# Where the query features of two tiles are made, which engine stores the gates, and one raw buffer fewer, in a fused gMLP and linear-attention kernel

## The chip, the cores and the metric

The kernel runs on one core of a Trainium2 chip. The metric is the time of one execution on the device, in microseconds (us). The core has TensorE (PE in the profile; its weight loads are PEld), VectorE (DVE), ScalarE (ACT), GpSimd (POOL) and SyncE (SP). Each engine has its own stream of instructions; they meet at semaphores. SP, ACT and POOL also start DMA transfers.

## What is computed

The reference, cut to what matters, with S = 2048 rows, D = 512 columns, H = 32 heads of 16, and 688 gated channels:

```python
xn = layernorm(x)
# A: linear attention
q, k, v = split_heads(xn @ wqkv)
phi(t) = concat(softmax(t @ w_phi), softmax(-(t @ w_phi)))      # per head, 32 features
o = phi(q) (phi(k)^T v) / (phi(q) sum(phi(k)) + 1e-6)
A = merge_heads(o) @ wo
# B: gated MLP with a spatial projection
z1, z2 = split(gelu(xn @ w_in))                                 # 688 + 688 channels
g = w_sp @ layernorm(z2) + b_sp                                 # over the 2048 rows
B = (z1 * g) @ w_out
return x + A + B
```

All is float32; each product of matrices is made of three matmuls over operands split into a rounded part and a rest.

## The kernel before

Rows are worked in 16 tiles of 128. A **pair** is two neighbouring tiles. The kernel has four stages.

1. **Attention inputs** (to about 200 us): layernorm, the projections of q, k and v, the two softmaxes of each. The unnormalised features of q (`e`, 128 x 1024 a tile, with the reciprocals of their sums) are stored to the DRAM tensor `e_d`; the raw z1 halves go to `z1_d`.
2. **Gate inputs** (to about 275 us): the sum of the key features `zb`, the z2 half with its gelu and layernorm, and the B operands of the spatial product. The **finished features** of tiles 0 and 1 (`NE = 2`) are made here: `q_fin` (lines 559 to 570) multiplies `e` by `zb`, sums per head (L563, L564), makes the quotient (L565 to L568) and scales `e` by it (L570). They go back to `e_d`.
3. **Spatial stage** (its products from 275 to 484 us): `w_sp @ z2` by Strassen-Winograd on 2 x 2 blocks. There are 8 pairs of output tiles, and each is worked in 4 **chunks**, so chunks 0 to 31. A chunk has seven products, P1, P2, P6, P5, P7, P3, P4, of six matmuls each of 344 columns (lines 57 to 59); the seven accumulate over the four chunks of a pair in seven PSUM buffers `g` of a pool of eight. In what follows 12P2 is product P2 of chunk 12.
4. **Output stage** (from about 484 us): for every pair of tiles the gated u times `w_out`, the attention by finished features, and its product with `wo`.

**What one chunk costs the other engines.** `load_a(n)` has SP load 512 KB of `w_sp` into a raw buffer `wf` (L607). `prep_a(n)` makes the left operands from it: ACT rounds (L49), DVE subtracts for the rest (L53) and forms the Winograd sums (L637 to L640). An A operand has four tiles: A11 with A12 (used by P1 and P2), A22 (P4), S2 with S1 (P6 and P5), S4 with S3 (P7 and P3). There are two sets of them, for even and odd chunks, so the tiles of chunk n + 2 are written only after the products of chunk n that read them.

**What one pair costs.** After the last chunk of pair i `drain` empties the seven `g` into `c`: ACT copies P1 (L835), DVE does the other seven steps (L834, L837, L838, L840). The next pair's P2 takes the buffer that P1 held, its P6 that of P2, and so on. `gate` applies gelu to z1, which POOL has loaded into `z1t` (L808, L850 on ACT), multiplies it by `c` (L853 on DVE), and `turn` transposes the product in 32 x 32 blocks into the same `z1t` (L862, L864) and stores it to DRAM (L868, L870), eight DMAs a pair. `c` and `z1t` have one buffer each.

**Turned features.** The attention wants the finished features transposed. For pair 0 (tiles 0, 1) and pairs 4 to 7 (`TQ = 8`) DVE transposes them in blocks and POOL stores them to `q_d` (`turn_q`, L579, L581), from where they are loaded turned. Tiles 0 and 1 are turned in the spatial stage after the gates of pairs 2 and 4: `e` comes into the buffer of `c`, its transpose goes to that of `z1t` (L966 to L968). Pairs 1 to 3 (tiles 2 to 7) are transposed by PE (`attend_T`, L1047, into `ptq`) and copied by ACT (L1049). Tile 2 is finished at chunk 29, tiles 3 to 15 in the output stage (`features`, from `ahead(i)`, three tiles ahead).

**What sets the order.** A scheduler orders each engine's instructions when the kernel is built, by times that it estimates; on the chip each engine then takes its instructions in that order. `in_turn` (L647) fixes by hand the order of named steps of DVE and ACT where the stages meet (chunks 1 to 8).

```python
if n + 4 < NC:
    raw[n + 4] = load_a(n + 4)          # three raw buffers: f, x, y
if 0 < n < NC - 2:
    A[n + 2] = prep_a(n + 2, raw.pop(n + 2))
```

Of the kernel before, what the change touches and what calls it, by code (L numbers as in the profile page):

```python
# [18 lines left out]
P = 128  # L19
# [22 lines left out]
def mixer(ctx: ExitStack, tc: tile.TileContext, x, x_t, wv, wqkT, phi_bd, wo, w_in, wst, b_r, w_out, out):  # L42
# [528 lines left out]

    TQ = 8

# [27 lines left out]
    def load_a(n):  # L601
        i, q = SEQ[n]
        tag = "fx"[n] if n < 2 else "fxy"[(n - 2) % 3]
        t = (fy[0] if tag == "y" else ws).tile([P, 2, QC, P], F32, tag="wf" + tag, name="wf")
        for k in range(2):
            with tc.issue_after(load_a.last) if n == 5 else ExitStack():
                load_a.last = sp.dma_start(t[:, k], wst[2 * i + k, :, q * QC:(q + 1) * QC, :]).ins  # L607
        return [t[:, k].rearrange("p (k two) t -> p two k t", two=2) for k in range(2)]
# [38 lines left out]
    def in_turn(*keys):  # L647
        for e in range(2):
            queue = [turns[k][e] for k in keys if e < len(turns[k])]
            for a, b in zip(queue, queue[1:]):  # L650
                tc.add_manual_dep(b, a.name, mybir.DependencyInfo(
                    mybir.DependencyClass.NoSync, mybir.DependencyReason.DATA), reason="order of the border")
# [177 lines left out]
    def drain(i, g, cb):  # L830
# [12 lines left out]
        for k, x in enumerate(steps + [drained]):  # L843
            turns["c", i, k] = x.ins,
        return cb, first.ins, drained.ins

    def gate(i, cb, z, u, ut, after=None):
        cb, first, _ = cb
        with tc.issue_after(after or first):
            act.activation(z[:, :, :FH], z[:, :, :FH], AF.Gelu_apprx_tanh)  # L850
        zs = z[:, :, :FH].rearrange("p k (j f) -> p k j f", j=2)
        us = u[:, :, :FH].rearrange("p k (j f) -> p k j f", j=2)
        dve.tensor_tensor(us, zs, cb, op=ALU.mult)  # L853
        lo, hi = u[:, :, KF * P:FH], u[:, :, FH:FU].bitcast(F32R)
# [3 lines left out]
        def turn():  # L858
            src = ut.rearrange("p k f -> p (k f)")
            m, r = src[:, :2 * KF * P], src[:, 2 * KF * P:]  # L860
            for k in range(2):
                dve.transpose(m[:, k * KF * P:(k + 1) * KF * P].rearrange("p (m c t) -> p m c t", c=KF, t=BL),  # L862
                              u[:, k, :KF * P].rearrange("p (c m j) -> p m c j", c=KF, j=BL))
            dve.transpose(r.rearrange("p (k f) -> p k f", k=2), u[:, :, KF * P:])  # L864
            eng = pool if i == NP - 2 else sp
            for b in range(0, P, BL):
# [51 lines left out]
    for n in range(NC):  # L918
# [5 lines left out]
        if n % NQ == NQ - 1 and i < NP - 1:  # L924
# [3 lines left out]
            g = {}  # L928
        if n + 4 < NC:
            raw[n + 4] = load_a(n + 4)  # L930
        if 0 < n < NC - 2:
            A[n + 2] = prep_a(n + 2, raw.pop(n + 2))
        if n == 6:
            in_turn((1, "sums"),
# [24 lines left out]
        if n % NQ == NQ - 1 and i < NP - 1:  # L959
            turn = gate(i, cb, z, c, z, prep_a.last)  # L960
            if i < NP - 2:
                turn()
            if i in (2, 4):
                s = i // 2 - 1
                e, t = (gt.tile([P, 2, FU], F32, tag=tag, name=name).rearrange("p k f -> p (k f)")[:, :NF]
                        for tag, name in (("c", "c"), ("z1", "z1t")))  # L966
                pool.dma_start(e, e_d[s, :, :NF])
                turn_q(s, t, e, pool)  # L968
        if n == NC - 4:
            stage_w()  # L970
        if n == NC - 3:
            zb = slot("zb")[:, :NF]
            sp.dma_start(zb, zb_d)
            uT = [first_gate(0)]
            ets[2] = load_q(2, slot("et"))
            es[2], last = q_fin(ets.pop(2), slot("qtmp")[:, :NF], zb)
        if n == NC - 2:
# [25 lines left out]
    def features(s):  # L1003
        with tc.issue_after(fin[-1]):
            tmp = slot("qtmp")[:, :NF]
# [117 lines left out]
    with tc.issue_after(load_w.last):  # L1123
        ets[3] = load_q(3, slot("et"))
        for s in (2, 3):
            us[s] = fetch_u(s)
        ets[4] = load_q(4, slot("et"))

    def ahead(i):

        if i + 5 < NT:
            ets[i + 5] = load_q(i + 5, slot("et"))
        if i + 4 < NT:
            with tc.issue_after(brought[i + 2]) if i + 6 >= NT else ExitStack():
                us[i + 4] = fetch_u(i + 4)
        if 3 < i + 3 < NT:
            features(i + 3)

    p, nxt = {}, dict(enumerate(uT))
    for i in range(0, NT, 2):  # L1140
# [65 lines left out]
```

## Time and profile before

| | |
|---|---|
| Median of 3 runs | 611.46 us (611.17 to 613.96) |
| The profiled execution | 612.24 us, of which the span of the instructions is 610.5 us |
| Busy in the span: PE, PEld, DVE, ACT, POOL | 99%, 90%, 86%, 43%, 22% |
| Mean granted clock of TensorE | 1.000 |
| DVE busy, 300 to 340 us, 340 to 380, 500 to 540 | 37.45, 32.99, 38.90 of 40 us |
| Data moved | 107.85 MB, 177 GB/s on average |

How to read it: times are microseconds from the span's start, means of a group are nanoseconds. In a group's row the numbers are busy time and mean, then the time that the engine stood idle just before these instructions and what ended most of it. In a timeline a row is an instruction with its start and duration; the idle time ahead of it, where there was any, stands in brackets with what ended it. Instructions of one engine overlap a little, so the distance between two starts is what one costs when the next doesn't wait. A busy PE is not PE at its peak, since matmuls are pipelined; the count of matmuls in a window says more.

### The profile page before, as it was taken

How to read it: one execution, taken by the hardware profiler on the slowest of the kernel's cores; microseconds unless marked ns; L12 is line 12 of the kernel's file. 1: busy time of each engine (PE TensorE's matmuls, PEld its weight loads, DVE VectorE, ACT ScalarE, POOL GpSimd, SP SyncE). 2: the span in 40 equal slices, each digit the busy share in tenths (PEclk: the TensorE clock that was granted, in tenths of full speed). 3: DMA queues.
4: the chain of work that ended last, by engine and by line, in shares of the span. 5: the costliest groups of instructions: out<-in, count | busy, mean ns of one | idle time of the engine just before them, and what ended most of it. 6: DMA issues, size and time to landing. Idle time of an engine off the chain costs nothing.

```text
span 610.5 us, 11382 instructions
## 1 busy us (share of the span) xinstructions
PE 602.8 (99%) x4286; PEld 548.5 (90%) x4286; DVE 525.4 (86%) x930; ACT 260.3 (43%) x414; POOL 131.8 (22%) x231
## 2 busy tenths in 40 slices
PE   8999999999999999999999999999999999999997
PEld 7888888888888999999999999999999988877775
DVE  5999999999987578989999897997998999999922
ACT  5643324423433547877434433443435343332220
POOL 4122332323111005442000001001100041153420
PEclk9999999999999999999999999999999999999999
DMA  8557876566537758002344736556664799699782
GB/s 315 193 130 178 217 176 188 145 168 165 144 96 221 241 201 306 5 1 65 121 107 135 208 104 173 163 154 161 176 185 154 228 299 292 191 326 248 183 236 67
DMA packets 57950, 107.85 MB, mean 177 GB/s; under 512 B 12392, under 2 KB 24552, under 8 KB 57672
## 3 DMA queue, kind: packets, MB, share of 16 engines
q1 hardware_dynamic: 43656, 65.22, 34.6%
q0 software_dynamic: 11936, 36.28, 24.2%
q10 hardware_dynamic: 2304, 5.64, 2.4%
q8 instruction: 33, 0.54, 0.4%
q14 instruction: 21, 0.17, 0.1%
HBM read 66.85 MB, written 35.54 MB: 168 GB/s over the span
## 4 chain that ended last, share of the span: by engine, by line
PE 82%; DVE 5%; ACT 4%; issue 4%; POOL 3%; DMA 1%; ACTq 0%; POOLq 0%; DVEq 0%
PE g L57 9%; PE g L59 9%; PE g L58 9%; PE proj L58 7%; PE proj L57 7%; PE proj L59 7%; PE pout L57 5%; PE pout L59 5%; PE pout L58 5%; PE zps L57 3%; PE zps L59 3%; PE zps L58 3%; PE po L1062 1%; DMA et<-e_d 1%; PE kvps L372 1%
## 5 line engine op out<-in xcount | busy, mean ns | idle before, releaser
L57 PE MATMUL g<-B,A 128*128 128x344 f32 x448 | 140.4, 317 | 0.9 <-ACT A L49 0.9
L58 PE MATMUL g<-B,A 128*128 128x344 f32 x448 | 141.1, 317 | 0.0
L59 PE MATMUL g<-B,A 128*128 128x344 f32 x448 | 135.5, 317 | 0.0
L49 ACT ACTIVATE A<-wf 128x512 fp32r<-128x512 f32 (+1 forms) x128 | 69.9, 573 | 109.5 <-DVE wf L639 64.8
L57 PEld LDWEIGHTS g<-B,A 128*128 128x128 f32 x448 | 83.8, 188 | 1.4 <-ACT A L49 1.4
L53 DVE TENSOR_TENSOR A<-wf,A 128x512 fp32r<-128x512 f32 (+1 forms) x128 | 76.5, 619 | 9.8 <-ACT A L49 9.4
L58 PEld LDWEIGHTS g<-B,A 128*128 128x128 f32 x448 | 84.0, 188 | 0.0
L59 PEld LDWEIGHTS g<-B,A 128*128 128x128 f32 x448 | 82.7, 188 | 0.3 <-DVE A L53 0.2
L57 PE MATMUL proj<-wqk_h,xT 128*128 128x512 f32 x128 | 50.1, 391 | 0.0
L59 PE MATMUL proj<-wqk_h,xT 128*128 128x512 f32 x128 | 49.8, 389 | 0.0
L58 PE MATMUL proj<-wqk_l,xT 128*128 128x512 f32 x128 | 49.8, 389 | 0.0
L124 ACT ACTIVATE e<-e,r_x 128x1024 f32<-128x1024 f32 x26 | 29.7, 1148 | 42.2 <-DVE e L123 41.2
L57 PE MATMUL zps<-w1h,xT 128*128 128x344 f32 (+2 forms) x128 | 40.9, 320 | 0.0
L59 PE MATMUL zps<-w1h,xT 128*128 128x344 f32 (+2 forms) x128 | 40.7, 318 | 0.0
L58 PE MATMUL zps<-w1l,xT 128*128 128x344 f32 (+2 forms) x128 | 40.7, 318 | 0.0
L57 PE MATMUL zps<-w2h,xT 128*128 128x344 f32 (+2 forms) x128 | 40.7, 318 | 0.0
L58 PE MATMUL zps<-w2l,xT 128*128 128x344 f32 (+2 forms) x128 | 40.6, 317 | 0.0
L59 PE MATMUL zps<-w2h,xT 128*128 128x344 f32 (+2 forms) x128 | 40.3, 317 | 0.0
L127 DVE TENSOR_REDUCE sm<-e 128x64 f32<-128x1024 f32 x26 | 31.1, 1199 | 2.5 <-ACT e L124 2.5
L808 POOL DMA_DIRECT2D z1t<-z_d x16 | 9.1, 594 | 105.3 <-DVE A L53 38.2
L57 PE MATMUL pout<-wu,uh 128*128 128x512 f32 x75 | 30.4, 406 | 0.0
L59 PE MATMUL pout<-wu,ul 128*128 128x512 f32 x75 | 29.3, 391 | 0.0
(217 smaller groups left out, 1373.0 us busy)
## 6 DMA issues: line engine op xcount, KB each, us to landing
wf<-in_wst SPq DMA_DIRECT2D x64, 256.0 KB, 3.8
e_d<-e POOLq DMA_DIRECT2D x16, 544.0 KB, 4.4
et<-e_d SPq DMA_DIRECT2D x16, 544.0 KB, 7.1
z_d<-z1f ACTq DMA_DIRECT2D x16, 344.0 KB, 2.9
z1t<-z_d POOLq DMA_DIRECT2D x16, 344.0 KB, 4.2
zacc<-e POOLq DMA_DIRECT2D x10, 512.0 KB, 4.8
u<-u_d SPq DMA_DIRECT2D x15, 320.0 KB, 4.9
xt<-in_x SPq DMA_DIRECT2D x16, 256.0 KB, 4.3
```

The lines of the kernel that those rows point to most:

```text
L49: return act.activation(h, src, AF.Copy).ins
L53: return (eng or dve).tensor_tensor(l, src, h.bitcast(F32), op=ALU.subtract).ins
L57: pe.matmul(dst, ah, bh, start=start, stop=False)
L58: pe.matmul(dst, ah, bl, start=False, stop=False)
L59: return pe.matmul(dst, al, bh, start=False, stop=stop).ins
L124: softmax_pair.last = less, act.activation(e, e, AF.Exp, scale=scale).ins
L127: dve.tensor_reduce(sm, heads(e), axis=AX.X, op=ALU.add)
L372: i = pe.matmul(kv_acc[k:k + QP, m // 4], vs[:, m * QP:(m + 1) * QP], e[:, m * HP:(m + 1) * HP], start=first and m < 4 and len(ready) == n ...
L808: pool.dma_start(t[:, k, :FH], z1_d[2 * i + k])
L1062: lasts[3] = pe.matmul(po[r][c * QP:(c + 1) * QP, k], kvT[rows, m // 2, cols], fs[m // 4][rows, m // 2 % 2], start=True, stop=True).ins
```

## The change

- **Features of tiles 2 and 3** are made and turned in the spatial stage. After the gates of pairs 1, 2, 3 and 4 come tiles 2, 0, 3 and 1. For tiles 2 and 3 `q_fin` runs there too, on `e` in the buffer of `c`, with scratch in that of `z1t` and with `zs`, a copy of `zb` that POOL loads at chunk 6. `TQ` becomes 6: pair 3 (tiles 6, 7) is turned by DVE and loaded turned like the pairs behind it, and pair 1 is loaded turned from `q_d`. Only pair 2 is left to PE's transposes. Tile 4 is finished at chunk 29; the output stage makes tiles 5 to 15, five tiles ahead.
- **One raw buffer fewer.** `zs` takes the third raw buffer, so from chunk 8 on two alternate, and the load of chunk n + 4 stands behind the preparation of chunk n + 2.
- **Stores of the gates**: POOL issues them for pairs 0 to 6, where SP did for pairs 0 to 5.
- **Orders**: at the border pair 0's copy of P1, its gelu, its gate's product and its transposes get fixed places, the last behind the preparation of chunk 7. From chunk 8 on only one thing is fixed: a chunk's S4 rest stands ahead of the next chunk's first sum on DVE.

```diff
-    TQ = 8
+    TQ = 6
...
-        tag = "fx"[n] if n < 2 else "fxy"[(n - 2) % 3]
+        tag = "fx"[n] if n < 2 else "fxy"[(n - 2) % 3] if n < 8 else "fx"[n % 2]
...
-            eng = pool if i == NP - 2 else sp
+            eng = pool if i < NP - 1 else sp
...
-        if n + 4 < NC:
+        if n < 6:
             raw[n + 4] = load_a(n + 4)
         if 0 < n < NC - 2:
             A[n + 2] = prep_a(n + 2, raw.pop(n + 2))
+        if 6 <= n < NC - 4:
+            raw[n + 4] = load_a(n + 4)
+        if n == 6:
+            zs = fy[0].tile([P, 2, QC, P], F32, tag="wfy", name="zs").rearrange("p a b c -> p (a b c)")
+            pool.dma_start(zs, zb_d)
...
-                    (6, "A11"), (6, "A22"), (6, "first"), (6, "sums"), (6, "S2"), (6, "S4"),
+                    (6, "A11"), (6, "A22"), ("z", 0), (6, "first"), (6, "sums"), (6, "S2"), (6, "S4"),
+                    ("u", 0),
                     (7, "A11"), (7, "A22"), (7, "first"), (7, "sums"), (7, "S2"), (7, "S4"),
+                    ("ut", 0, 0), ("ut", 0, 1),
...
-            if i in (2, 4):
-                s = i // 2 - 1
-                e, t = (gt.tile([P, 2, FU], F32, tag=tag, name=name).rearrange("p k f -> p (k f)")[:, :NF]
+            if 0 < i < 5:
+                s = (2, 0, 3, 1)[i - 1]
+                e, t = (gt.tile([P, 2, FU], F32, tag=tag, name=name).rearrange("p k f -> p (k f)")
                         for tag, name in (("c", "c"), ("z1", "z1t")))
-                pool.dma_start(e, e_d[s, :, :NF])
+                t = t[:, :NF]
+                if s < NE:
+                    e = e[:, :NF]
+                    pool.dma_start(e, e_d[s, :, :NF])
+                else:
+                    e, _ = q_fin(load_q(s, e[:, :QW], pool), t, zs)
                 turn_q(s, t, e, pool)
...
-            ets[2] = load_q(2, slot("et"))
-            es[2], last = q_fin(ets.pop(2), slot("qtmp")[:, :NF], zb)
+            ets[4] = load_q(4, slot("et"))
+            es[4], last = q_fin(ets.pop(4), slot("qtmp")[:, :NF], zb)
...
+    for n in range(8, NC - 6):
+        in_turn((n, "S4"), (n + 1, "first"))
...
-        if 3 < i + 3 < NT:
-            features(i + 3)
+        if 0 < i < NT - 5:
+            features(i + 5)
```

**The order that it makes.** Before, on DVE where pair 2 is drained into `c_4071`: `wf_3885` is chunk 12's raw buffer, `wf_3949` chunk 13's, and the `g` of L834 to L840 are the pair's products.

```order
L640 TENSOR_TENSOR wf_3885<-wf_3885 128x2x128
L53 TENSOR_TENSOR A_4016<-wf_3885,A_4016 128x2x256
L834 SCALAR_TENSOR_TENSOR c_4071<-g_3843,bias_78,c_4071 128x344
L53 TENSOR_TENSOR A_4013<-wf_3885,A_4013 128x2x256
L53 TENSOR_TENSOR A_4085<-wf_3949,A_4085 128x2x256
L837 TENSOR_TENSOR c_4071<-g_3850,c_4071 128x344
L838 TENSOR_TENSOR c_4071<-g_3857,c_4071 128x344
L834 SCALAR_TENSOR_TENSOR c_4071<-g_3864,bias_78,c_4071 128x344
L840 TENSOR_TENSOR c_4071<-g_3864,c_4071 128x344
```

The drain stands among the last steps of chunk 12's preparation, ahead of nearly all of chunk 13's. Now, on DVE at the same drain (`c_4088`): `wf_3982` is chunk 13's raw buffer, `c_3838` holds the `e` of tile 2 and is the same single buffer as `c_4088`.

```order
L640 TENSOR_TENSOR wf_3982<-wf_3982 128x2x128
L53 TENSOR_TENSOR A_4100<-wf_3982,A_4100 128x2x256
L53 TENSOR_TENSOR A_4097<-wf_3982,A_4097 128x2x256
L563 TENSOR_TENSOR z1t_3839<-c_3838,zs_3751 128x1024
L564 TENSOR_REDUCE c_3838<-z1t_3839 128x64
L565 TENSOR_TENSOR c_3838<-c_3838 128x64
L566 SCALAR_TENSOR_TENSOR c_3838<-c_3838 128x32
L567 RECIPROCAL c_3838<-c_3838 128x32
L568 TENSOR_TENSOR c_3838<-c_3838 128x64
L570 TENSOR_TENSOR c_3838<-c_3838 128x1024
L579 STREAM_TRANSPOSE z1t_3839<-c_3838 128x1024
L834 SCALAR_TENSOR_TENSOR c_4088<-g_3860,bias_78,c_4088 128x344
```

The whole preparation of chunk 13 and the features of tile 2 now stand ahead of the drain of pair 2. At the drain of pair 4 it is the same with chunk 21 and tile 3; at those of pairs 3 and 5 only the transpose (L579) of tiles 0 and 1 stands just ahead. On PE the scheduler has moved products too: a chunk's P4 comes early, and between the last matmul of 7P4 and the first of 12P2 stand 204 matmuls; from the last of 11P4 to 12P2 stand 36, from 12P2 to 14P4 84, from 14P4 to 14P6 23, from 16P2 to 18P6 104 with 19P4 at 102, and from 18P6 to 20P2 64.

Before, on POOL from the load of pair 2's z1 to that of pair 4's:

```order
L808 DMA z1t_3904<-z1_d_64 128x688 x2
L967 DMA c_4114<-e_d_63 128x1024
L581 DMA q_d_69<-z1t_4115 32x4x256 x4
L808 DMA z1t_4190<-z1_d_64 128x688 x2
L808 DMA z1t_4468<-z1_d_64 128x688 x2
```

Now, on POOL from the load of pair 1's z1 to the stores of pair 2's gate:

```order
L808 DMA z1t_3626<-z1_d_64 128x688 x2
L870 DMA u_d_65<-z1t_3626 32x8x160 x4
L872 DMA ur_d_66<-z1t_3626 32x6x32 x4
L556 DMA c_3838<-e_d_63 128x1088
L581 DMA q_d_69<-z1t_3839 32x4x256 x4
L808 DMA z1t_3921<-z1_d_64 128x688 x2
L870 DMA u_d_65<-z1t_3921 32x8x160 x4
```

Eight stores stand ahead of the load of `e`, and the load of pair 2's z1 stands behind the stores of tile 2's turned features, which leave from the same buffer.

More of the change, by code (lines that the diff above doesn't have):

```diff
@@ L553, in mixer, with load_q @@
     QW = NF + 7 * H
-    def load_q(s, et):
-        sp.dma_start(et[:, :NF + 2 * H], e_d[s])
+    def load_q(s, et, eng=None):
+        (eng or sp).dma_start(et[:, :NF + 2 * H], e_d[s])
         return et
@@ L648, in in_turn @@
         for e in range(2):
-            queue = [turns[k][e] for k in keys if e < len(turns[k])]
+            queue = [turns[k][e] for k in keys if e < len(turns[k]) and turns[k][e]]
             for a, b in zip(queue, queue[1:]):
@@ L844, in drain @@
             turns["c", i, k] = x.ins,
+        turns["c12", i] = None, first.ins
         return cb, first.ins, drained.ins
@@ L849, in gate @@
         with tc.issue_after(after or first):
-            act.activation(z[:, :, :FH], z[:, :, :FH], AF.Gelu_apprx_tanh)
+            turns["z", i] = None, act.activation(z[:, :, :FH], z[:, :, :FH], AF.Gelu_apprx_tanh).ins
         zs = z[:, :, :FH].rearrange("p k (j f) -> p k j f", j=2)
         us = u[:, :, :FH].rearrange("p k (j f) -> p k j f", j=2)
-        dve.tensor_tensor(us, zs, cb, op=ALU.mult)
+        turns["u", i] = dve.tensor_tensor(us, zs, cb, op=ALU.mult).ins,
         lo, hi = u[:, :, KF * P:FH], u[:, :, FH:FU].bitcast(F32R)
@@ L861, in turn @@
             for k in range(2):
-                dve.transpose(m[:, k * KF * P:(k + 1) * KF * P].rearrange("p (m c t) -> p m c t", c=KF, t=BL),
-                              u[:, k, :KF * P].rearrange("p (c m j) -> p m c j", c=KF, j=BL))
+                turns["ut", i, k] = dve.transpose(
+                    m[:, k * KF * P:(k + 1) * KF * P].rearrange("p (m c t) -> p m c t", c=KF, t=BL),
+                    u[:, k, :KF * P].rearrange("p (c m j) -> p m c j", c=KF, j=BL)).ins,
             dve.transpose(r.rearrange("p (k f) -> p k f", k=2), u[:, :, KF * P:])
-            eng = pool if i == NP - 2 else sp
+            eng = pool if i < NP - 1 else sp
             for b in range(0, P, BL):
@@ L945, in mixer @@
                     (3, "S4"),
[1 row of a table removed]
+                    (4, "A11"), (4, "A22"), ("c12", 0), (4, "first"), (4, "sums"),
                     ("c", 0, 0),
@@ L1003, in features @@
     def features(s):
-        with tc.issue_after(fin[-1]):
+        with tc.issue_after(fin[-1]), tc.issue_after(lasts[7]):
             tmp = slot("qtmp")[:, :NF]
@@ L1123, in mixer @@
     with tc.issue_after(load_w.last):
[L1124 to L1127, printed above, removed]
+        ets[5] = load_q(5, slot("et"))
+        us[2] = fetch_u(2)
+        ft[2] = f_pair()
+        for k in range(2):
+            sp.dma_start(ft[2][:, k], q_d[2 + k])
+        us[3] = fetch_u(3)
+        ets[6] = load_q(6, slot("et"))
     def ahead(i):
-        if i + 5 < NT:
-            ets[i + 5] = load_q(i + 5, slot("et"))
+        if i + 7 < NT:
+            ets[i + 7] = load_q(i + 7, slot("et"))
         if i + 4 < NT:
-            with tc.issue_after(brought[i + 2]) if i + 6 >= NT else ExitStack():
+            with tc.issue_after(brought[i + 4]) if i + 6 >= NT else ExitStack():
                 us[i + 4] = fetch_u(i + 4)
-        if 3 < i + 3 < NT:
-            features(i + 3)
+        if 0 < i < NT - 5:
+            features(i + 5)
     p, nxt = {}, dict(enumerate(uT))
@@ L1153, in mixer @@
             fin.append(lasts[7])
-            features(3)
+            features(5)
             with tc.issue_after(fin[-1]), tc.issue_after(lasts[8]):
```

1 row of the table g is left out of this document.

## The prediction

> **What bounds the kernel now.** First the page, then the windows, then PE's timeline for what it loses.
>
> ```profile
> span 610.5 us, 11382 instructions
> PE 602.8 (99%) x4286; PEld 548.5 (90%) x4286; DVE 525.4 (86%) x930; ACT 260.3 (43%) x414; POOL 131.8 (22%) x231
> PEclk9999999999999999999999999999999999999999
> ```
>
> PE is busy nearly everywhere at full clock, and DVE is next. By windows (after the stretch: PE, PEld, DVE, ACT, POOL busy, with counts):
>
> ```profile
> 300.00:340.00 40.00, 39.12 (x250) 38.35 (x250) 37.45 (x76) 16.00 (x29) 1.06 (x2) 1.00 0.45 129
> 340.00:380.00 40.00, 40.00 (x261) 39.95 (x260) 32.99 (x70) 16.02 (x28) 3.81 (x7) 1.00 0.58 156
> 380.00:420.00 40.00, 40.00 (x262) 40.00 (x261) 36.81 (x76) 16.69 (x29) 2.70 (x5) 1.00 0.55 155
> 500.00:540.00 40.00, 40.00 (x276) 31.70 (x275) 38.90 (x61) 14.90 (x27) 9.78 (x15) 1.00 0.86 249
> ```
>
> In the spatial stage 262 matmuls in 40 us are 0.153 us each, with no gap: PE sets the pace. A chunk's 42 are 6.4 us, a pair's 168 are 25.7. DVE has 3 to 7 us left in 40. At the border (300 to 340) 12 matmuls are missing, 1.8 us; two waits are seen:
>
> ```profile
> 303.54 0.39 PE L57 MATMUL g<-B,A 128*128 128x344 f32 x1 [0.25 <-ACT A L49]
> 318.52 0.43 PE L57 MATMUL g<-B,A 128*128 128x344 f32 x1 [0.64 <-ACT A L49]
> ```
>
> So work taken from PE counts in full; work given to DVE is free only where nothing that PE needs soon is queued behind it.
>
> **What it takes away.** In the chain that ended last, two pairs of the output stage, one with PE's transposes and one without:
>
> ```profile
> 520.15 0.93 PE pout L1083 x4
> 531.18 1.75 PE ptq L1047 x16
> 536.34 0.93 PE pout L1083 x4
> 550.99 0.93 PE pout L1083 x4
> ```
>
> From one L1083 to the next it is 16.2 us with `ptq` and 14.65 without; two of three go: 2 x 1.75 = 3.5 us, all on PE's path. ACT's eight copies and the output stage's DVE work fall too (13 `q_fin` and 8 transposes become 11 and 10), which was hidden. Features five tiles ahead instead of three give their round trip through DRAM more time; I count 0.5 us of small waits. The border's fixed places I credit with the two waits, 0.9 us (0 to 1.8). Together 4.9 us (3.5 to 6.4). Moving tile 4 in for tile 2 at chunk 29 changes nothing: the same instructions. The third raw buffer I cost at nothing while DVE keeps pace: a load lands in 3.8 us and a chunk lasts 6.4; it bites only where DVE catches up (within the bounds below).
>
> **What it adds: DVE's price list.** The timeline of DVE at the drain of pair 3 and the gate behind it, where what costs is the distance between starts:
>
> ```profile
> 377.34 0.42 DVE L637 TENSOR_TENSOR wf<-wf 128x256 f32<-128x256 f32 x1
> 377.80 0.43 DVE L638 TENSOR_TENSOR wf<-wf 128x256 f32<-128x256 f32 x1
> 378.14 0.57 DVE L834 SCALAR_TENSOR_TENSOR c<-g,bias,c 128x344 f32<-128x344 f32 x1
> 378.63 0.42 DVE L639 TENSOR_TENSOR wf<-wf 128x256 f32<-128x256 f32 x1
> 378.96 0.69 DVE L53 TENSOR_TENSOR A<-wf,A 128x512 fp32r<-128x512 f32 x1
> 379.56 0.51 DVE L837 TENSOR_TENSOR c<-g,c 128x344 f32<-128x344 f32 x1
> 379.99 0.42 DVE L640 TENSOR_TENSOR wf<-wf 128x256 f32<-128x256 f32 x1
> 386.73 1.29 DVE L53 TENSOR_TENSOR A<-wf,A 128x512 fp32r<-128x512 f32 x2 [0.30 <-ACT A L49]
> 388.50 1.59 DVE L853 TENSOR_TENSOR c<-z1t,c 128x1376 f32<-128x1376 f32 x1 [0.47 <-ACT z1t L850]
> 390.01 0.42 DVE L53 TENSOR_TENSOR A<-wf,A 128x256 fp32r<-128x256 f32 x1
> 390.34 0.20 DVE L855 CAST c<-c 128x96 fp32r<-128x96 f32 x1
> 390.46 1.57 DVE L862 STREAM_TRANSPOSE z1t<-c 128x640 f32<-128x640 f32 x2
> 391.95 0.39 DVE L637 TENSOR_TENSOR wf<-wf 128x256 f32<-128x256 f32 x1
> ```
>
> A rest of 512 columns 0.60, of 256 0.33; a sum 0.33 to 0.46, say 0.42; a drain step 0.43 or 0.49, seven 3.25; the gate's product 1.51, its transposes 1.49, with its small steps 3.6. A `q_fin` is the distance from one L563 to the next:
>
> ```profile
> 500.01 1.22 DVE L563 TENSOR_TENSOR qtmp<-et,zb 128x1024 f32<-128x1024 f32 x1
> 504.79 1.22 DVE L563 TENSOR_TENSOR qtmp<-et,zb 128x1024 f32<-128x1024 f32 x1
> L579 DVE STREAM_TRANSPOSE z1t<-c 128x1024 f32<-128x1024 f32 x2 | 2.5, 1246 | 5.9 <-DMA wf<-in_wst 5.9
> L835 ACT ACTIVATE c<-g 128x344 f32<-128x344 f32 x8 | 3.6, 445 | 1.0 <-issue 0.6 <-PE g L59 0.5
> ```
>
> So 4.8, and 1.25 for the transpose: a tile made and turned is 6.05 us, about what DVE has to spare in a pair. What matters is where it is queued. Of the 5.9 us in L579's row most is this wait (behind the brackets the next chunk's L639 stands queued and doesn't run):
>
> ```profile
> 369.25 0.42 DVE L638 TENSOR_TENSOR wf<-wf 128x256 f32<-128x256 f32 x1
> 373.03 1.25 DVE L579 STREAM_TRANSPOSE z1t<-c 128x1024 f32<-128x1024 f32 x1 [3.36 <-DMA wf<-in_wst]
> 374.20 0.38 DVE L639 TENSOR_TENSOR wf<-wf 128x256 f32<-128x256 f32 x1
> ```
>
> **Term 1, drain of pair 2.** 12P2 needs the PSUM buffer that ACT's L835 empties into `c`; now `c` still holds tile 2's `e` until L579 is through, and ahead of it stands chunk 13's preparation. Count from the end of 7P4, where A22 of chunk 9 may first be written. PE has 204 matmuls x 0.153 = 31.2 us. DVE has, in the order, 16 rests of 512 (9.6), 5 of 256 (1.7), 24 sums (10.1), a drain (3.25), a gate (3.6), `q_fin` and transpose (6.05): 34.3. With ACT's rounding ahead (0.42) and L835 behind (0.44) it is 35.2, and waits on ACT like the 0.30 above, up to six, bring it to 36.2. PE waits 36.2 - 31.2 = **5.0 us** (4 without any wait; 7 if DVE comes late out of the border).
>
> **Term 2, gate of pair 2.** POOL loads pair 3's z1 only when the turned features have left `z1t`. Before, this chain ran once after L579 of 373.03:
>
> ```profile
> 374.57 2.22 POOL L581 DMA_DIRECT2D q_d<-z1t  x4 [7.66 <-DVE wf L639]
> 381.28 1.10 POOL L808 DMA_DIRECT2D z1t<-z_d  x2 [4.50 <-DMA wf<-in_wst]
> 387.12 1.34 ACT L850 ACTIVATE z1t<-z1t 128x1376 f32<-128x1376 f32 x1
> ```
>
> From the end of L579 (374.28) to the gate (388.50) are 14.2 us. Now L579 ends 0.44 ahead of 12P2, so the gate starts 13.8 after it; A22 of chunk 14 is queued behind and ready 1.9 later, at 15.7. PE reaches 14P4 after 84 x 0.153 = 12.8: 2.9 lost. 14P6 follows after 23 (3.5 us) but S2 of chunk 14 comes 6.4 after the gate's start: 1.0 more. **3.9 us** (0 if the chain takes 11 us or less; 6).
>
> **Terms 3 and 6, drains of pairs 3 and 5**, where only a transpose is ahead. The drain is late by about 0.8. Then the same 14.2: A22 of chunk 19 is ready 13.8 + 3.8 = 17.6 after 16P2 and PE is there after 102 x 0.153 = 15.6; 2.0 lost, and 0.9 at 18P6. **3.7 us** (0 to 5), for pair 5 4.0 (0 to 7).
>
> **Term 4, drain of pair 4.** From the gate of pair 3 to L579 of tile 3 DVE has the gate (3.6), 14 sums (5.9), 10 rests of 512 (6.0), 3 of 256 (1.0) and the tile (6.05): 22.6, with L835 and waits 23.5. PE starts 18P6 5.0 after that gate and has 64 matmuls (9.8) to 20P2: 23.5 - 14.8 = **8.7 us** (6.5 to 10). **Term 5**, its gate: as term 2, 3.9 (0 to 6).
>
> The loads of `e` must be there by then. Eight stores are now ahead of them on POOL:
>
> ```profile
> L868 POOL DMA_DIRECT2D u_d<-z1t x4 | 2.3, 594 | 37.8 <-DVE z1t L864 37.8
> u_d<-z1t POOLq DMA_DIRECT2D x4, 160.0 KB, 6.1
> c<-e_d POOLq DMA_DIRECT2D x2, 512.0 KB, 5.3
> ```
>
> 8 x 0.59 + 0.5 + 5.3 = 10.5 us after the transposes, while DVE has about 11.6 of other work: just in time, so I add nothing.
>
> **Sum.** 5.0 + 3.9 + 3.7 + 8.7 + 3.9 + 4.0 = 29.2 lost, 4.9 won: +24.3. The profiled execution took 612.24 (span 610.5 and 1.7 around it), so 636.5; the median of the runs is 0.8 lower: I forecast **635.5 us**, with 617 to 649 from the ends of the terms (10.5 lost and 4.9 won; 41 and 3.5).
>
> [...] The clock's row has 9 in every slice, and PE's longest wait quoted from the stage is 0.64 us, so what the clock does over 5 to 9 us isn't in this trace. [...]
>
> **The rivals.**
>
> - *Hidden after all.* The scheduler's places hold, PE never waits, only the 4.9 stay: 606.6 us, faster. For it: 3 to 7 us of DVE idle in every 40. Against it: DVE's 35.2 would have to fit in 31.2, 11% less than its rows. Chance 0.11.
> - *Only the two drains.* The z1 chain is shorter than 14.2 (L850 may have been ACT's own order, not the load: z1's second load was issued by 382.4), and terms 2, 3, 5, 6 shrink to the late drains, 0.8 each for pairs 3 and 5: 612.2 + 5.0 + 8.7 + 1.6 - 4.9 - 0.8 = 622. Chance 0.25.
> - *POOL is late.* The stores land in 6.1 and hold up the loads of `e`; each of the four comes 2 us later than DVE wants it: 643.5. For it: the margin of 1 us. Chance 0.12.
> - [...] Chance 0.12.
>
> **How the numbers follow.** 0.40 for the forecast, 0.25, 0.12, 0.12 and 0.11 for the rivals. A measurement here can tell about 0.5%, 3 us. All but the first rival are slower by more: slower 0.87; of the first nearly all is faster, 606.6 being 0.8% below: faster 0.10, same 0.03. The range leaves out the hidden case and the far ends: 615 to 648.
>
> **What would show it.** In the profile of after: PE idle before L57 of `g` released by ACT `c` L835, one wait of about 5 us near 360 and one of about 9 near 415 to 430; behind each, a wait on ACT or DVE `A` of 2 to 4 us; DVE idle before L854 by ACT `z1t`; 16 `ptq` matmuls; POOL with some 48 more DMAs between 310 and 470. Of the products before:
>
> ```profile
> L57 PE MATMUL g<-B,A x448: 313/316/427, 275.4 to 483.7; 128*128 128x344 f32 x150
> ```
>
> I am wrong if this stage (208.3 us) stays under 215, or if PE waits but for `wf` or `e` instead of L835.

## The result and the profile after

The changed kernel takes **663.9 us** (median of 5 runs, 662.3 to 665.0) against 611.5 (5 runs): **1.0848 times as long, 95% interval 1.0829 to 1.0867**. Slower, as forecast, but by 52 us instead of 24, and outside the range of 615 to 648. The profiled execution has a span of 660.3 against 610.5: 49.8 us to be found.

The page of after, the lines that answer to the prediction's first fence:

```profile
span 660.3 us, 11307 instructions
PE 615.5 (93%) x4254; PEld 555.2 (84%) x4254; DVE 531.9 (81%) x934; ACT 256.4 (39%) x406; POOL 169.9 (26%) x298
PEclk9999999999999999999998799969799989999989
```

PE is busy for 93% of the span instead of 99, and its clock, 9 in all 40 slices before, dips in several. No other engine has become the bound: DVE fell from 86% to 81%. PE waits for something. Where, the windows say: the spatial stage and what follows it, of after and then of before (PE, PEld, DVE, ACT, POOL busy with counts, granted clock, DMA share, GB/s).

```profile
275.60:524.70 249.10, 218.89 (x1345) 214.07 (x1344) 194.43 (x383) 90.64 (x159) 50.97 (x92) 0.93 0.45 135
524.70:660.30 135.60, 123.23 (x751) 95.80 (x749) 97.67 (x148) 33.68 (x54) 40.61 (x64) 0.96 0.82 235
```

```profile
275.40:484.00 208.60, 207.72 (x1344) 206.90 (x1344) 185.82 (x375) 91.93 (x161) 17.64 (x33) 1.00 0.54 154
484.00:610.50 126.50, 121.56 (x783) 96.26 (x781) 100.50 (x154) 37.08 (x61) 36.27 (x56) 1.00 0.79 226
```

The spatial stage is 40.5 us longer and the output stage 9.1: together all of it. The same 1344 products (one is counted twice at the edge) keep PE busy for 218.9 us instead of 207.7. So the 40.5 are 29.3 us more of idle time (30.2 against 0.9) and 11.2 us in which PE is busy longer with the same matmuls, in part at a lower clock (0.93 over the stage against 1.00). PE's timeline in after, its longer waits in both stages:

```profile
366.24 0.66 PE L57 MATMUL g<-B,A 128*128 128x344 f32 x1 [10.07 <-ACT c L835]
396.10 0.42 PE L57 MATMUL g<-B,A 128*128 128x344 f32 x1 [1.02 <-ACT c L835]
425.54 0.42 PE L57 MATMUL g<-B,A 128*128 128x344 f32 x1 [2.89 <-ACT A L49]
437.28 0.66 PE L57 MATMUL g<-B,A 128*128 128x344 f32 x1 [9.72 <-ACT c L835]
468.61 0.65 PE L57 MATMUL g<-B,A 128*128 128x344 f32 x1 [2.62 <-ACT c L835]
540.02 0.79 PE L57 MATMUL pout<-woh,oT 128*128 128x512 f32 x1 [3.38 <-ACT oT L49]
634.54 0.64 PE L57 MATMUL pout<-woh,oT 128*128 128x512 f32 x1 [3.13 <-ACT oT L49]
```

The four waits for L835 are the drains of pairs 2, 3, 4 and 5, where terms 1, 3, 4 and 6 put them. The others are new. DVE's and ACT's rows ahead of the first long wait, and a later one, show what the forecast had costed at nothing: a wait for the raw chunk `wf`.

```profile
347.98 1.63 DVE L53 TENSOR_TENSOR A<-wf,A 128x512 fp32r<-128x512 f32 x3 [1.40 <-ACT A L49]
354.52 1.63 DVE L53 TENSOR_TENSOR A<-wf,A 128x512 fp32r<-128x512 f32 x3 [2.06 <-ACT A L49]
407.14 0.94 ACT L49 ACTIVATE A<-wf 128x512 fp32r<-128x512 f32 x2 [6.31 <-DMA wf<-in_wst]
```

ACT rounds a chunk before DVE takes its rest; when the chunk has not landed, both stand still, and all that is queued behind them, drains and gates too. The chain of waits of after between 430 and 500 us joins it all (start, length, what):

```profile
435.49 1.26 DVE z1t L579
...
438.66 2.85 DMA q_d<-z1t
442.61 3.47 DMA z1t<-z_d
446.30 1.36 ACT z1t L851
...
458.29 5.31 DMA wf<-in_wst
...
466.91 1.17 DVE z1t L579
```

From the turn (L579) the path runs through the store of the turned features, the load of the next z1 into the same buffer and the gelu; then through a late chunk to the next turn (466.91), behind which the same chain runs again. Three resources, each in short supply by the change: the buffer `z1t`, the buffer `c` (the waits for L835), and two raw buffers instead of three.

### The profile page after: what moved, and what is told of

The parts are those of the page before. It is cut to its first block, busy times and chain, and to the rows that moved or that the text cites. A ratio compares the mean times of both kernels' runs of the same rounds, so it can differ in the third digit from the quotient of the medians.

```text
span 660.3 us, 11307 instructions
## 1 busy us (share of the span) xinstructions
PE 615.5 (93%) x4254; PEld 555.2 (84%) x4254; DVE 531.9 (81%) x934; ACT 256.4 (39%) x406; POOL 169.9 (26%) x298
## 5 line engine op out<-in xcount | busy, mean ns | idle before, releaser
L57 PE MATMUL g<-B,A 128*128 128x344 f32 x448 | 145.3, 328 | 28.8 <-ACT c L835 23.4
L58 PE MATMUL g<-B,A 128*128 128x344 f32 x448 | 144.3, 324 | 0.0
L59 PE MATMUL g<-B,A 128*128 128x344 f32 x448 | 134.5, 325 | 1.4 <-DVE A L53 1.1
L57 PEld LDWEIGHTS g<-B,A 128*128 128x128 f32 x448 | 86.5, 193 | 32.2 <-ACT c L835 24.7
L58 PEld LDWEIGHTS g<-B,A 128*128 128x128 f32 x448 | 86.7, 194 | 0.0
L59 PEld LDWEIGHTS g<-B,A 128*128 128x128 f32 x448 | 84.2, 193 | 2.8 <-DVE A L53 2.8
L57 PE MATMUL proj<-wqk_h,xT 128*128 128x512 f32 x128 | 50.2, 392 | 0.0
L57 PE MATMUL zps<-w1h,xT 128*128 128x344 f32 (+2 forms) x128 | 40.9, 321 | 0.0
L57 PE MATMUL zps<-w2h,xT 128*128 128x344 f32 (+2 forms) x128 | 40.7, 318 | 0.0
L870 POOL DMA_DIRECT2D u_d<-z1t x28 | 16.4, 592 | 92.4 <-DVE et L568 38.7
L57 PE MATMUL pout<-woh,oT 128*128 128x512 f32 x60 | 25.6, 426 | 6.5 <-ACT oT L49 6.5
```

The lines of the kernel that those rows point to most:

```text
L57: pe.matmul(dst, ah, bh, start=start, stop=False)
L58: pe.matmul(dst, ah, bl, start=False, stop=False)
L59: return pe.matmul(dst, al, bh, start=False, stop=stop).ins
L870: eng.dma_start(u_d[2 * i:2 * i + 2, :, w:w + KF * BL].rearrange("k (m j) w -> j (k m) w", j=BL), m[b:b + BL].rearrange("p (m w) -> p m w" ...
```

## The experiments

Each kernel is after with one thing changed, unless it says otherwise. "Stage" is from the first to the last L57 of `g`: 208.3 us in before, 248.8 in after. Ratios are to before, which ran between them (medians 611.6 to 612.2). In raw3, own_e, own_t and own_both `zs` isn't kept: `q_fin` multiplies the tile by itself instead, the same instruction on the same shape, so these four time the change and do not compute its result. The edits of own_e and own_both move the later lines of the kernel by three, so that L838 there is L835 of after.

**The added features left out (nofeat).**

```diff
-            if 0 < i < 5:
-                s = (2, 0, 3, 1)[i - 1]
+            if i in (2, 4):
+                s = i // 2 - 1
...
-            sp.dma_start(ft[2][:, k], q_d[2 + k])
+            sp.dma_start(ft[2][:, k], q_d[k])
```

> After with the features of tiles 2 and 3 left out of the spatial stage: only tiles 0 and 1 are turned there, after pairs 2 and 4 as in before; the output stage loads their features for tiles 2 and 3 as well, so its work is that of after. Two raw buffers, stores by GpSimd and the border stay. Theory A: no drain waits, so only the last tiles' late u load (about 5 us) stands against the transposes and the border: 608 to 613 us. Theory B: DVE has time again, but the loads are still issued two chunks ahead: waits for wf of some us and an output stage that starts late, 616 to 626 us.

621.9 us, ratio 1.0178 (1.0147 to 1.0209). Its stage:

```profile
L57 PE MATMUL g<-B,A x448: 313/316/655, 275.9 to 491.6; 128*128 128x344 f32 x150
```

215.7 us. So the added features with their loads and places cost 33.1 of the 40.5, and 7.4 stay without them: theory B for what is left.

**Two raw buffers alone, on before (twobuf).**

```diff
-        tag = "fx"[n] if n < 2 else "fxy"[(n - 2) % 3]
+        tag = "fx"[n] if n < 2 else "fxy"[(n - 2) % 3] if n < 8 else "fx"[n % 2]
...
-        if n + 4 < NC:
+        if n < 6:
             raw[n + 4] = load_a(n + 4)
         if 0 < n < NC - 2:
             A[n + 2] = prep_a(n + 2, raw.pop(n + 2))
+        if 6 <= n < NC - 4:
+            raw[n + 4] = load_a(n + 4)
```

> Before with two raw buffers from chunk 8 on instead of three, each chunk loaded after the preparation that frees its buffer; nothing else. As the prediction had it (a third buffer costs nothing while DVE keeps pace): 611 to 613 us. If two buffers alone are what the kernel without the added features lost in its spatial stage (215.7 us against 208.3): 617 to 622 us.

621.7 us, 1.0165 (1.0145 to 1.0186): **10.0 us for a buffer that I had costed at nothing.** The waits of twobuf by engine and line (us, times, longest):

```profile
ACT A L49 <- DMA wf<-in_wst: 51.2, 23, 5.4
DVE A L53 <- ACT A L49: 21.4, 34, 2.4
```

and the same two in before:

```profile
ACT A L49 <- DMA wf<-in_wst: 2.2, 3, 1.1
DVE A L53 <- ACT A L49: 9.4, 29, 1.4
```

In before ACT waits for `wf` for 2.2 us in all. With two buffers a chunk is issued only when the chunk two before it has been prepared, and DVE, which had 3 to 7 us in 40 to spare, waits 12.0 us more for ACT's roundings (21.4 against 9.4).

**Three raw buffers again, without the added features (nofeat3).** The edits of nofeat and of raw3 below, together.

> The kernel without the added features, with three raw buffers again: left of the change are the stores by GpSimd, the fixed orders, the output stage. If two buffers made that kernel's loss, its 7.4 us in the spatial stage go, and the output stage starts no later than in before: 611 to 614 us, of which 5 are the last u loads. If GpSimd's stores or the fixed orders made it: 618 to 622 us.

615.7 us (612.4 to 618.0), 1.0061 (1.0040 to 1.0081); the profiled one has a span of 610.7.

```profile
L57 PE MATMUL g<-B,A x448: 313/316/423, 276.2 to 483.8; 128*128 128x344 f32 x150
```

The stage is 207.6 us, even 0.7 under before. In this run GpSimd's stores and the fixed orders cost nothing there; the two buffers made nofeat's loss in the stage (8.1 us). But the profiled run is the fastest of eight. The median is 1.7 us above what was expected and 3.3 us above that run; why stays open.

**Three raw buffers, with the features (raw3).**

```diff
-        tag = "fx"[n] if n < 2 else "fxy"[(n - 2) % 3] if n < 8 else "fx"[n % 2]
+        tag = "fx"[n] if n < 2 else "fxy"[(n - 2) % 3]
...
-                    e, _ = q_fin(load_q(s, e[:, :QW], pool), t, zs)
+                    e, _ = q_fin(load_q(s, e[:, :QW], pool), t, e[:, :NF])
```

> After with the third raw buffer given back: each chunk's load is issued four chunks ahead again, as in before. To make room the normaliser's z is left out: the features of tiles 2 and 3 multiply the tile by itself instead, the same instruction on the same shape. Theory A (what is queued on DVE ahead of the drains, and the turned features that hold z1t, make the loss): the two long waits for L835 stay near 10 us each; only the waits for wf go (2.9 us at chunk 19 and up to 5 of the 10.1 at pair 2): 655 to 661 us. Theory B (two raw buffers make the greater part of what the forecast missed: chunks come late, and the loads of w_out, u and wo, which stand behind them on SP, too): the first wait falls to 5, the second to 8, the ones for wf go, the start of the output stage gives back 4 to 8: 638 to 648 us.

652.5 us, 1.0660 (1.0636 to 1.0684), 11.4 less than after. PE's two long waits and the stage:

```profile
365.35 0.66 PE L57 MATMUL g<-B,A 128*128 128x344 f32 x1 [9.61 <-ACT c L835]
435.32 0.65 PE L57 MATMUL g<-B,A 128*128 128x344 f32 x1 [9.87 <-ACT c L835]
L57 PE MATMUL g<-B,A x448: 313/316/656, 275.5 to 518.3; 128*128 128x344 f32 x150
```

The long waits stay, as theory A said; theory B had them at 5 and 8. The time lies between the two, below the 655 of A. The stage gives back 6.0 us and what lies behind it 3.6. So the third buffer is worth some 10 us in all with the features as without, and it isn't what makes the drains late.

**The made tile not in the gate's `c` (own_e).**

```diff
-                e, t = (gt.tile([P, 2, FU], F32, tag=tag, name=name).rearrange("p k f -> p (k f)")
-                        for tag, name in (("c", "c"), ("z1", "z1t")))
-                t = t[:, :NF]
+                e = fy[0].tile([P, QW], F32, tag="wfy", name="e")
+                t = gt.tile([P, 2, FU], F32, tag="z1", name="z1t").rearrange("p k f -> p (k f)")[:, :NF]
```

> After with the tile that is made lying in a tile of its own (in the place of the third raw buffer, which stays away) instead of in the gate's c: no drain waits for a turn of features any more. The normaliser's z is left out as in the other kernel (the tile is multiplied by itself). Theory A: the four late drains go (10.1 + 9.7 + 1.0 + 2.6 = 23.4 us of waits for L835, and the slow matmuls behind them), the gates' chain by z1t stays: 632 to 642 us. Theory B: the waits for wf stay and show where the drains stood before: 648 us or more.

642.9 us, 1.0515 (1.0480 to 1.0549), 21.0 less than after and 0.9 above the range of theory A.

```profile
389.07 0.65 PE L57 MATMUL g<-B,A 128*128 128x344 f32 x1 [6.24 <-ACT c L838]
455.48 0.66 PE L57 MATMUL g<-B,A 128*128 128x344 f32 x1 [8.30 <-ACT c L838]
L57 PE MATMUL g<-B,A x448: 313/316/656, 275.5 to 510.0; 128*128 128x344 f32 x150
```

The waits at pairs 2 and 4 (near 366 and 437) are gone: they were the tile in `c`. But two others stand at pairs 3 and 5: `z1t` is still held by the turned features, the gate of the pair before comes late, and the drain stands behind that gate, which also uses `c`. The lock has moved on to the next buffer.

**The turned features not in `z1t` (own_t).**

```diff
-                e, t = (gt.tile([P, 2, FU], F32, tag=tag, name=name).rearrange("p k f -> p (k f)")
-                        for tag, name in (("c", "c"), ("z1", "z1t")))
-                t = t[:, :NF]
+                e = gt.tile([P, 2, FU], F32, tag="c", name="c").rearrange("p k f -> p (k f)")
+                t = fy[0].tile([P, 2, QC, P], F32, tag="wfy", name="t").rearrange("p a b c -> p (a b c)")
```

> After with the turned features in a tile of their own (in the third raw buffer's place), so that the next pair's z1 is loaded without waiting for them; the tile itself still lies in the gate's c, so the drains still wait for the turn. The normaliser's z is left out (the tile is multiplied by itself). If the chain by z1t (terms 2, 3, 5, 6 of the forecast) costs PE time, the waits for A behind the late drains and the waits for L835 at pairs 3 and 5 (1.0 and 2.6) go: 650 to 656 us. If the chain was short enough to be hidden behind the drain (it took 11.3 us in after, not 14.2), nothing goes: 660 to 665. The two waits of about 10 us stay in both.

637.9 us, 1.0438 (1.0387 to 1.0489), 26.0 less than after: far more than either side had expected.

```profile
363.44 0.66 PE L57 MATMUL g<-B,A 128*128 128x344 f32 x1 [8.04 <-ACT c L835]
424.85 0.66 PE L57 MATMUL g<-B,A 128*128 128x344 f32 x1 [7.82 <-ACT c L835]
L57 PE MATMUL g<-B,A x448: 313/316/656, 275.8 to 502.8; 128*128 128x344 f32 x150
```

Of all waits of over 0.3 us only the two drains behind q_fin are left, and the stage has lost 21.8 us. With the same two raw buffers PE hardly waits for chunks here (0.3 us). I read it so that gates which come early leave DVE the time, and that what the chain by `z1t` costs is mainly this knock-on, not the wait right behind the gate; the two long waits, in which DVE can catch up, may have a part in it.

**Both taken away (own_both).** As own_e, and the turned features in that same tile (`t = e[:, :NF]`).

> After with the made tile and its turned features both in one tile of their own (in the third raw buffer's place), so that neither the gate's c nor z1t is held by them. To fit, work is falsified, not left out: q_fin multiplies the tile by itself in place, and the turn is made in place; the instructions, their shapes and the DMAs are those of after, the features of tiles 0 to 3 are wrong. Theory, the two holds make all that the added features cost in the spatial stage: it lasts as long as without the features, 215.7 us (213 to 220), and the whole 621 to 628 us. Rival, DVE's 12.1 us of added work (and the two raw buffers) costs by itself: 635 us or more.

632.4 us, 1.0333 (1.0310 to 1.0356). No wait for L835 is left, but 13 short ones of 0.2 to 2.1 us for `A`, 13.8 together, behind chunks that came late:

```profile
ACT A L49 <- DMA wf<-in_wst: 51.6, 25, 4.6
L57 PE MATMUL g<-B,A x448: 313/316/488, 275.8 to 502.3; 128*128 128x344 f32 x150
```

It lies between the two expectations: the stage is 226.5 us. The two holds made 22.3 of the 33.1. Of these own_t had won 21.8 by `z1t` alone: with `c` free as well, its two waits of 15.9 us together are gone, and yet the stage is but 0.5 us shorter, since 13.8 us of short ones came in their place (in the profiled runs, of which own_t's is the fastest of four; the medians are 5.5 us apart). So a wait that the trace shows is not what is gained when it goes. The other 10.8 (226.5 against 215.7 without the features) I put down to DVE's added work on top of two raw buffers. That is not shown by itself: ACT's waits for `wf` are as long in twobuf (51.2), the added loads and stores stay too, and a third raw buffer beside this was not tried.

**Turns without q_fin (turnonly).**

```diff
-                if s < NE:
-                    e = e[:, :NF]
-                    pool.dma_start(e, e_d[s, :, :NF])
-                else:
-                    e, _ = q_fin(load_q(s, e[:, :QW], pool), t, zs)
+                e = e[:, :NF]
+                pool.dma_start(e, e_d[s, :, :NF])
```

> After with the features of tiles 2 and 3 turned as they are: q_fin, 4.8 us of DVE a tile, is left out (those two tiles' output is not normalised), everything else stays, c and z1t are held as long by loads and turns. Theory A, DVE's time ahead of the drain is what costs: the waits at pairs 2 and 4 fall from 10.1 and 9.7 to those of pairs 3 and 5 (1.0 and 2.6), the slow matmuls behind them go as well: 636 to 644 us. Rival: c held from the load on costs, whatever DVE does with it: 652 us or more.

650.3 us, 1.0622 (1.0597 to 1.0648), only 13.6 less, nearer to the rival than to theory A. All four drains now wait alike:

```profile
360.81 0.66 PE L57 MATMUL g<-B,A 128*128 128x344 f32 x1 [2.31 <-ACT c L835]
396.34 0.65 PE L57 MATMUL g<-B,A 128*128 128x344 f32 x1 [4.04 <-ACT c L835]
430.02 0.65 PE L57 MATMUL g<-B,A 128*128 128x344 f32 x1 [1.96 <-ACT c L835]
465.43 0.66 PE L57 MATMUL g<-B,A 128*128 128x344 f32 x1 [3.58 <-ACT c L835]
```

It lies between the two. Ten us of arithmetic less bring the waits at pairs 2 and 4 down from 10.1 and 9.7 to 2.3 and 2.0, as theory A said, yet the stage is 242.9: those at pairs 3 and 5 have grown, and waits for `A` up to 2.6 us stand between. So most of the cost stays with the buffers held as before and the arithmetic gone.

**The last u loads (tail).**

```diff
-            with tc.issue_after(brought[i + 4]) if i + 6 >= NT else ExitStack():
+            with tc.issue_after(brought[i + 2]) if i + 6 >= NT else ExitStack():
```

> After with the loads of u for tiles 14 and 15 issued after the turned features of tiles 12 and 13 again, as in before, instead of 14 and 15. If they were late because they stood on SP behind loads that waited for GpSimd's stores, the last pair's interval falls from 19.5 to 14.4 us: 659 us (658 to 660). If the DMA engines' load held them up (their share is near full there), the time stays at 663 to 665.

656.8 us, 1.0738 (1.0716 to 1.0759): 7.1 less, more than the 5 expected (5.1 of it in the last pair's interval). In after SP and ACT show why:

```profile
618.13 7.15 SPq L1028 DMA_DIRECT2D f<-q_d  x2
625.40 0.43 SPq L888 DMA_DIRECT2D u<-u_d  x1
633.27 0.74 ACT L49 ACTIVATE uh<-u 128x640 fp32r<-128x640 f32 x1 [10.16 <-DMA u<-u_d]
```

A load of turned features that waits for GpSimd's stores holds SP for 7 us, and u of tile 14 is issued behind it; ACT waits 10.16 us for u with the rounding of `oT` queued behind, and PE for that (3.13 at 634.54). With the old order the last pair follows after 14.4 us (626.8 to 641.2) instead of 19.5 (626.7 to 646.2). This line is part of the change, and I gave it no term.

**A repaired kernel (own_t_tail).** own_t and tail together, the whole computation: z is loaded into `t` ahead of each q_fin.

```diff
+                    pool.dma_start(t, zb_d)
-                    e, _ = q_fin(load_q(s, e[:, :QW], pool), t, zs)
+                    e, _ = q_fin(load_q(s, e[:, :QW], pool), t, t)
```

> The whole computation: after with the turned features in a tile of their own, the normaliser's z loaded into that tile ahead of each q_fin instead of being kept, and the u loads of tiles 14 and 15 issued as in before. If the two gains add up (26.0 and 7.1 us): 629 to 633 us. If the tail's gain was already in the first (its last interval is 19.6 us there, so it should not be): 636 to 639 us. It stays slower than before, since the two drains still wait for their tiles (8.0 and 7.8 us and the slow matmuls behind).

634.2 us, 1.0367 (1.0344 to 1.0389). It lies between the two cases. PE has no wait at the last pairs any more, so the tail's gain is there, but the stage is 230.1 us against own_t's 227.0 (the wait at pair 2 is 10.0 instead of 8.0, that at pair 4 6.4 instead of 7.8), so the two don't quite add.

**u ahead of the turned features (u_first).** From own_t_tail, one statement moved:

```diff
+        us[3] = fetch_u(3)
         ft[2] = f_pair()
         for k in range(2):
             sp.dma_start(ft[2][:, k], q_d[2 + k])
-        us[3] = fetch_u(3)
```

> The repaired kernel (turned features in a tile of their own, u loads of the last tiles as before) with u of tile 3 loaded ahead of the turned features of tiles 2 and 3 on SP. If the wait of 2.7 us behind ACT's copy of tile 0's output (ACT stands ahead of it on a round of u that waits for its load) comes from that order: 630 to 632.5 us, 2 to 4 less, the wait gone. If DMA transport itself is full there: 634 as before.

631.1 us, 1.0316 (1.0298 to 1.0334): 3.1 less; the wait is gone and the first pair's interval falls from 19.0 to 15.0 us. The order of loads on SP was the cause, at this end of the stage too.

**The border's fixed orders alone, on before (border).** The new keys `c12`, `z`, `u`, `ut` in the list at chunk 6, nothing else.

> Before with only the fixed orders at the border (the gelu, the gate, its transposes and the copy of P1 of pair 0 added to the list). Forecast of this term: 0.9 us won (0 to 1.8), so 610 to 611.5 us; in the profile the two waits of 0.25 and 0.64 before chunk 8 go, and 261 or 262 matmuls instead of 250 start between 300 and 340 us. If the places cost as much elsewhere: 612 or more.

610.9 us, 0.9987 (0.9971 to 1.0003): 0.9 us less as forecast, but the interval holds 1, so the time alone doesn't tell it from no change. The window of the border in this kernel:

```profile
300.00:340.00 40.00, 40.00 (x262) 40.00 (x261) 37.51 (x78) 16.78 (x30) 1.06 (x2) 1.00 0.43 132
```

262 matmuls instead of 250: the waits are gone, as credited.

**Pair 3 loaded turned, without touching the spatial stage (pair3).** border, TQ = 6, features four tiles ahead:

```diff
-        if 3 < i + 3 < NT:
-            features(i + 3)
+        if i + 4 < NT:
+            features(i + 4)
```

> The fixed orders at the border, and pair 3 (tiles 6 and 7) loaded turned, with the features made four tiles ahead instead of three; pair 1 stays with PE's transposes, nothing is added to the spatial stage, three raw buffers stay. Forecast of the term: 1.75 us of ptq less on PE's path, on top of the border: 607.5 to 609.5 us. If the round trip of the features through DRAM comes too late for pair 3 (about 12 us against two tiles of 7.2), PE waits there instead: 611 or more.

623.2 us, 1.0184 (1.0159 to 1.0209), the second case:

```profile
541.32 1.96 PE L1066 MATMUL po<-f,kvT 64*32 64x256 f32 x32 [5.51 <-DMA f<-q_d]
```

The round trip of the features comes too late for pair 3 (5.51 us of waiting, and 5.16 more for a later pair at 576.85), and it costs more than the transposes that it saves.

**Tiles 2 and 3 finished early (early).** own_t_tail with NE = 4, so no q_fin in the spatial stage.

> The whole computation, with the features of tiles 2 and 3 finished where those of 0 and 1 are (ahead of the B operands, near 220 us), so that the spatial stage has four turns and no q_fin; turned features in a tile of their own, u loads of the last tiles as in before, two raw buffers. If the spatial stage can take the turns alone once nothing holds z1t, its 208 to 216 us stay, and the 3.5 us of ptq are won: 606 to 616 us, with up to 10 more if DVE has no room for 9.6 us of q_fin near 220 (it idles 3.4 us of the 20 from 220 on): up to 626. If c held by the tile costs by itself, waits for L835 of 2 to 4 us stay at all four drains, as in the kernel that only turns: 625 to 632 us.

644.7 us, 1.0507 (1.0449 to 1.0565): a miss. Its runs spread from 639.9 to 651.2 and the profiled one is the longest, so I read places in it and not sizes:

```profile
235.80 1.23 DVE L563 TENSOR_TENSOR qtmp<-et,zb 128x1024 f32<-128x1024 f32 x1 [7.06 <-DMA et<-e_d]
240.11 0.66 PE L57 MATMUL zps<-w2h,xT 128*128 128x344 f32 x1 [8.72 <-ACT z L776]
```

I had counted DVE's free time near 220, but not that the tile shares one load buffer with the one before: DVE stands 7 us in front of its load, all that is queued behind it stands too, and PE waits 8.7 us. The products begin 15 us later than in own_t_tail (290.8 against 275.4). Nor is the stage shorter without `q_fin` (229.8 us against 230.1): PE waits for L835 at all four drains (2.2, 2.0, 2.0 and 1.6 us), as the third case had it, so `c` held by the tile costs here too.

## Why the prediction was wrong

**Right: what bounds the kernel, the sign, the places.** PE pays for what DVE delivers late; the long waits are for L835 at pairs 2 and 4 (10.07 and 9.72 us), and they go when `c` isn't held (own_e). The loads of `e` held nothing up: ahead of the two L563 on `c` DVE stood for 0.3 us in all, and not for a DMA. The border's 0.9 is 0.9, and an interval without `ptq` is 14.4 us instead of 16.2.

**Term 4, 8.7 us, measured 9.72: near, in part by luck.** From the gate of pair 3 (409.66) to the end of L835 behind tile 3's turn (437.24) DVE and ACT took 27.6 us instead of 23.5, since DVE stood before late roundings. But PE had waited 2.89 us for `A` as well and came to 20P2 after 17.9 us instead of 14.8. Two errors of 4.1 and 3.1 us nearly cancel.

**Term 1, 5.0 us, measured 10.07.** The mechanism stands; the sum allowed DVE 1.0 us of waits on ACT between 7P4 and the drain. The window over that stretch of after:

```profile
324.10:364.80 40.70, 31.69 (x203) 30.85 (x201) 33.49 (x67) 12.92 (x23) 7.30 (x13) 0.92 0.48 147
```

DVE is busy for 33.5 us, what I had counted (34.3), but idle for 7.2, of which 3.46 stand in the two rows quoted above, before chunks that hadn't landed. Yet raw3, with three buffers, waits 9.61 there too: DVE stands 1.85 and 2.73 us before roundings in that stretch, the second time again for a chunk that hadn't landed. So the step that failed is a sum of durations with hardly any idle time, more than the buffer.

**"The third raw buffer I cost at nothing": failed.** It costs 10.0 us by itself (twobuf). "A load lands in 3.8 us and a chunk lasts 6.4" was true and beside the point: with two buffers the load is issued when a preparation ends, and DVE's preparations come in uneven order, between drains and gates. In after it costs behind the stage too, where raw3 takes 132.3 us instead of 135.9; twobuf loses nothing there (125.9 against 126.8 in before).

**Terms 2, 3, 5, 6, the chain by `z1t`, 15.5 us together.** From the end of L579 to the gate the chain took 11.3, 14.1, 10.9 and 12.9 us at pairs 2 to 5, where I had 14.2; the 14.1 has a late chunk ahead of the gelu on ACT (the 6.31 above). Right behind its gate at pair 2 PE waited for nothing, the zero that term 2 allowed. But taking the hold away gained 21.8 us of stage (own_t). I priced the chain at the next A22 and stopped; the gate's delay travels on in DVE's queue to the next preparation, the next raw load and the next drain, which own_e shows as waits of 6.2 and 8.3 us.

**The clock behind the waits: no term of the sum.** PE after its first long wait, and the window over the next 5.8 us and the 6 behind:

```profile
366.69 0.49 PE L58 MATMUL g<-B,A 128*128 128x344 f32 x1
366.98 0.49 PE L59 MATMUL g<-B,A 128*128 128x344 f32 x1
...
366.20:372.00 5.80, 5.76 (x20) 5.76 (x21) 4.77 (x9) 1.26 (x2) 2.81 (x6) 0.51 0.37 90
372.00:378.00 6.00, 6.00 (x41) 6.00 (x40) 1.01 (x1) 1.66 (x2) 0.26 (x1) 1.00 0.37 117
```

Twenty matmuls take 5.8 us instead of 3.1, 2.7 lost. The same stretch behind the waits of 9.72 us (pair 4) and 2.62 us (pair 5):

```profile
437.20:443.00 5.80, 5.72 (x28) 5.72 (x29) 4.78 (x9) 1.29 (x3) 2.94 (x6) 0.74 0.36 93
468.50:474.30 5.80, 5.69 (x20) 5.69 (x21) 5.46 (x12) 1.84 (x4) 3.07 (x6) 0.50 0.58 170
```

That is 1.5 and 2.7 lost: 6.9 us in the three. Behind terms 1 and 4 it is 4.2. A slow restart stood among the rivals, with a chance of 0.12, as a guess that no trace of before showed, and not in the sum; it came on top. The size of it differed: 2.7 us behind waits of 10.07 and 2.62 us, 1.5 behind one of 9.72. The rest of the 11.2 was not taken apart: twobuf's PE is busy 3.8 us longer than before's at a mean granted clock of 0.999 over the run.

**The output stage: 4.0 us won (3.5 of `ptq`, 0.5 of small waits) were 9.1 lost.** The transposes' gain is real, but two ends that I hadn't priced took more: the last u loads behind `f` on SP (tail), and the start, where the interval of the first pair is 22.6 us (530.2 to 552.8) against 16.2. There u came late because of SP's order in the repaired kernel (u_first); in after PE waited for `oT` (3.38), which stood on ACT behind a round of `wo` that waited 4.3 us for its load, and then ran at half pace (matmuls of 512 columns 0.43 us apart instead of 0.23, granted clock 0.50). That `wo` was late because SP's queue was is likely, but was not tried by itself.

**How the parts stand.** In the stage: 33.1 us for the added features (22.3 by the two holds, 10.8 that I put down to DVE's work on two raw buffers), 7.4 for two raw buffers net of the border's orders. These are differences between kernels whose orders differ too, so they are shares of this way of taking apart and no fixed prices. No version that turns more features beat before; the border's orders alone, at 0.9987, can't be told from it.

## What to carry to other kernels

When a step borrows a buffer, price how long it holds it, from the load into it to the last DMA out, and follow every instruction that this puts off through its engine's queue until the delay is absorbed; durations alone (here turnonly's 10 us of DVE) say little, and so does the longest wait that the trace shows (own_both). A prefetch buffer is not free because a load fits into a step (10.0 us in twobuf): test the kernel with one fewer before giving it away. And every line of a diff that changes what a load is issued after is a term of the sum, priced with what stands behind it on that queue.

## What the runs showed of the hardware

In after PE ran at half clock for 2.75 to 5.8 us behind five of its waits, of 2.62 to 10.07 us. After the 10.07 us the granted clock was 0.51 for 5.8 us and the matmuls of 344 columns started 0.29 us apart instead of 0.153; after the 9.72 us it was 0.50 for 2.75 us (437.28 to 440.03), and from 440.27 on they started 0.16 us apart. Behind the wait of 3.38 us at 540.02 those of 512 columns started 0.43 apart instead of 0.23; the window over it shows the clock:

```profile
540.00:545.80 5.80, 5.78 (x14) 4.53 (x15) 5.59 (x10) 1.93 (x3) 0.00 (x0) 0.50 1.02 395
```

The shortest wait of these is the 2.62 us at 468.61 (0.50 for 5.8 us). Behind the 1.02 us at 396.10 the granted clock was 1.00, and behind the 2.09 us at 434.35 in twobuf the matmuls started 0.16 us apart.

The many waits of 0.2 to 2.1 us in own_both brought its clock down little (0.994 over the run, against 0.965 in after). That did not make them cheap. Beside 13.8 us of them PE is busy with the stage's products for 212.9 us, 5.2 more than in before; in own_t, beside two waits of 15.9 us together, for 211.0, 3.3 more. What the busy time grows by at full clock was not taken apart.
